# Two more pairs' keys loaded in 32x32 blocks and turned by VectorE, with a new written order of all steps

## The chip, the cores and the metric

The kernel runs on one core of one Trainium2 chip. The core has a matrix engine (TensorE, PE in the profile, with its weight loads shown apart as PEld), three element engines (VectorE or DVE, ScalarE or ACT, GpSimd or POOL) and a queue engine (SyncE or SP) that issues most DMA transfers here. The five run their own instruction lists in order and wait for each other by semaphores. The metric is the device time of one execution in microseconds.

## The reference

Inputs are q, k and v of shape (4, 8, 768, 64) and two weight matrices, 512x2048 and 2048x512. For each of 4 batches the reference computes a block-sparse attention, then a Fourier mixing layer with a two-layer network on the result.

```python
k_rep = k.reshape(B, H, 12, 64, D).mean(axis=3)            # mean key of each block of 64
gate  = einsum('bhsd,bhnd->bhsn', q, k_rep)                # causal blocks only
mask  = (top 3 blocks of each query by gate) or (own block), and causal
attn  = softmax(where(mask, q @ k.T / 8, -1e9)) @ v
x     = attn with its 8 heads side by side                 # (4, 768, 512)
u     = x + real(fft(fft(x, axis=1), axis=2))
un    = (u - mean(u)) / sqrt(var(u) + 1e-6)
out   = u + maximum(un @ w_ch1, 0) @ w_ch2
```

## The kernel before

**Units of work.** Two heads of one batch make a pair; there are 16 pairs (P = 0 to 15), four to a batch. For each pair the kernel needs q and k with the 64 elements of a head along the partitions, while memory holds them with the elements along a row. It has two ways to turn them.

- By TensorE: `load` fetches a whole head in rows of 64 floats (line 282, two transfers of 192 KB), `a_tp` (steps `tk` for keys and `tq` for queries, line 297) turns it in six 128x128 transposes into PSUM, and the later steps read PSUM.
- By blocks: `load` fetches 32 rows by 32 columns at a time (line 277, four transfers of 96 KB, rows of 32 floats), so that a turn within 32x32 blocks finishes the job. For keys that turn is `k_turn` (step `kb`, line 301), a VectorE instruction in place in SBUF; for queries it is `a_q32` (step `qc`, line 326), which copies to a new tile as well.

`BLK` on line 203 says which pairs go by blocks: queries from pair 7 on, keys from pair 9 on.

**Attention of a pair.** From the turned keys VectorE takes block sums (`a_sums`, step `ks`, line 306) and `kh` spreads them for the two heads; ScalarE casts the keys to 16 bits (`a_k`, step `kc`, lines 317 and 320), GpSimd the queries (`a_q`, step `qs`). TensorE computes gate scores (`g`); VectorE turns them (`gt`), finds the top values (`gx`, nine or ten MAX8 instructions), compares (`gl`, two instructions) and turns the mask back (`gm`). From pair 7 on GpSimd writes the mask into the operand of the scores (`K`). TensorE computes six score tiles (`s`), ScalarE takes the exponentials (`e`), GpSimd cuts the diagonal (`d`), TensorE multiplies by v (`v`, line 461; `vc` casts v on GpSimd) and VectorE divides (`x`, line 472 and a product).

**Mixing of a batch.** VectorE folds the four pairs' x (`fs`, `fd`, then `f:b,0` to `f:b,3`, lines 504 to 516). TensorE multiplies by the Fourier tables along the sequence (`y`, line 531), ScalarE and VectorE copy out (`ty`, `tr`), TensorE multiplies along the features (`m`), VectorE adds x (`u`) and ScalarE scales to 16 bits (`xu`). The result is turned into the tile `unT` (`un`): in batch 0 by TensorE (`xt`) and a VectorE copy (line 602), in the other batches by DMA transposes on SP (line 605). VectorE also takes the statistics (`bn`, `nv`), GpSimd finishes them (`nr`).

**The network.** 16 steps `w` of a batch (lines 641 and 643) multiply `unT` by the first weights, `r` applies the maximum (ScalarE, every fourth on VectorE, line 651), 12 half-steps `c` (line 668) multiply by the second weights, `o` adds on VectorE and `od` stores.

**Order.** The string `ORDER` (lines 112 to 177) is a list of these steps, written out and recorded one after the other with the framework's own scheduling switched off. So it gives each engine its instruction list: an engine runs its parts of the steps in the order of the list, and a step that must wait holds up all later ones on the same engine. SP's loads and stores stand in the same list (`Lk`, `Lq`, `Lv` for keys, queries and values, `LT` and `LF` for the Fourier tables). All PSUM results come from one pool of four buffers, so a fifth result waits for the first to be read; the q and k rows as loaded have three buffers each.

Of the kernel before, what the change touches and what calls it, by code (L numbers as in the profile page):

```python
# [112 lines left out]
Lk:1 Lq:1 Lk:2 Lq:2 tk:0 ks:0 tq:0 Lq:3 Lk:3 kh:0 qc:0 iz:1 tk:1 qs:0 kc:0 g:0 ks:1 iz:0 gt:0 tq:1  # L113
kc:1 gx:0 Lq:4 Lv:0 Lk:4 Lv:1 kh:1 gl:0,0 tk:2 gl:0,1 gm:0 kc:2 qc:1 s:0,3 s:0,2 ks:2 e:0,3 qs:1
tq:2 Lq:5 Lk:5 s:0,5 qc:2 g:1 e:0,5 e:0,2 kh:2 s:0,4 gt:1 qs:2 s:0,0 e:0,4 gx:1 s:0,1 d:0,2 tq:3
gl:1,0 e:0,0 gl:1,1 tk:3 gm:1 e:0,1 d:0,0 qc:3 g:2 d:0,3 kc:3 d:0,5 s:1,5 gt:2 d:0,4 s:1,0 e:1,5
qs:3 ks:3 s:1,4 e:1,0 tq:4 d:0,1 gx:2 vc:0 e:1,4 s:1,3 qc:4 s:1,1 Lv:2 e:1,3 s:1,2 gl:2,0 kh:3 tk:4
gl:2,1 e:1,2 d:1,3 gm:2 g:3 d:1,4 ks:4 d:1,0 v:0 d:1,5 gt:3 vc:1 kc:4 gx:3 e:1,1 s:2,5 Lv:3 Lq:6
LF:0 Lq:7 Lk:6 Lk:7 LT:0 s:2,3 kh:4 gl:3,0 e:2,5 gl:3,1 s:2,4 e:2,3 d:1,1 x:0 tq:5 qs:4 e:2,4 g:4
d:2,3 gm:3 qc:5 s:2,0 d:2,4 s:2,2 d:1,2 e:2,0 gt:4 d:2,5 tk:5 vc:2 gx:4 e:2,2 s:2,1 ks:5 d:2,0 Lv:4  # L120
Lq:8 Lk:8 s:3,1 e:2,1 v:1 gl:4,0 kh:5 gl:4,1 kc:5 d:2,1 gm:4 d:2,2 s:3,2 x:1 e:3,1 vc:3 g:5 e:3,2
Lv:5 Lc:0 d:3,1 s:3,5 gt:5 s:3,0 fs:0,1 e:3,5 s:3,3 d:3,2 gx:5 e:3,0 s:3,4 fs:1,1 tq:6 gl:5,0 e:3,3
fs:0,0 v:2 gl:5,1 fs:1,0 e:3,4 d:3,3 qc:6 d:3,0 s:4,5 x:2 d:3,4 s:4,4 e:4,5 d:3,5 s:4,0 qs:5 v:3
e:4,0 gm:5 fs:2,0 fs:2,1 e:4,4 s:5,5 x:3 s:4,1 e:5,5 s:5,1 e:4,1 fd:2,0 s:4,2 s:5,0 fs:3,1 e:5,1
# [41 lines left out]
d:14,0 vc:14 v:15 w:2,13 w:2,11 r:2,13 v:14 r:2,11 w:2,6 r:2,14 w:2,0 w:2,9 w:2,2 w:2,5 r:2,9 r:2,2
# [15 lines left out]
def kernel(  # L182
# [617 lines left out]
```

## Time and profile before

| What | Value |
|---|---|
| Median of 3 runs | 292.67 us (292.5 to 293.05) |
| The profiled execution's own time | 292.97 us |
| Its span from first to last instruction | 291.2 us |
| TensorE busy | 276.6 us (95%) |
| VectorE busy | 202.9 us (70%) |
| ScalarE busy | 163.6 us (56%) |
| GpSimd busy | 116.1 us (40%) |
| Granted TensorE clock | 1.0 of full speed throughout |

The profile is one execution. Its page gives busy time by engine, the same in 40 slices, the chain of work that ended last (each piece was released by the one before it), groups of like instructions, and DMA issues. Other answers of the trace give the instructions in order of time, sums over chosen stretches, and the time from a transfer's issue to its landing. Matmuls are pipelined, so their mean duration is longer than the distance from one to the next.

### The profile page before, as it was taken

What the parts mean: (1) busy time and instruction counts of PE and PEld (TensorE: products, weight loads), DVE (VectorE), ACT (ScalarE), POOL (GpSimd) and SP (SyncE); (2) the same over time, 40 slices, a digit from 0 to 9 for tenths busy, and PEclk for the clock granted to TensorE, in tenths of its full rate; (3) what the DMA queues carried; (4) which work ended last, traced back from release to release, by engine and by line L of the source; (5) the groups of instructions that cost most, each with busy time, mean ns of one, the idle gap of its engine ahead of it and who ended that gap; (6) DMA issues with size and microseconds to landing.
All of it is one profiled execution on the core that took longest, in us unless ns stands there. A gap on an engine that the chain in (4) does not pass through costs nothing.

```text
span 291.2 us, 6585 instructions
## 1 busy us (share of the span) xinstructions
PE 276.6 (95%) x2537; PEld 169.2 (58%) x2537; DVE 202.9 (70%) x604; ACT 163.6 (56%) x205; POOL 116.1 (40%) x286
## 2 busy tenths in 40 slices
PE   8799999899998989999998999999999999999994
PEld 4466777655665465556574466656676454564642
DVE  2999999999996978977899766793566155420231
ACT  3698989865872625978577672864263401353100
POOL 2267527454888650852771798038000000003000
PEclk9999999999999999999999999999999999999999
DMA  9999999998999297259610002543000331000063
GB/s 199 278 225 228 205 200 205 221 170 155 172 174 194 65 222 131 51 123 242 109 41 2 0 7 50 146 91 146 0 2 0 37 109 36 0 2 0 0 237 127
DMA packets 118287, 33.52 MB, mean 115 GB/s; under 512 B 111024, under 2 KB 115056, under 8 KB 118256
## 3 DMA queue, kind: packets, MB, share of 16 engines
q1 hardware_dynamic: 112592, 28.47, 45.0%
q0 software_dynamic: 3664, 4.19, 8.8%
q10 hardware_dynamic: 2000, 0.44, 0.7%
q8 instruction: 20, 0.33, 0.5%
q14 instruction: 11, 0.09, 0.1%
HBM read 28.63 MB, written 6.29 MB: 120 GB/s over the span
## 4 chain that ended last, share of the span: by engine, by line
PE 68%; DVE 17%; ACT 8%; POOL 4%; issue 2%; DVEq 0%; ACTq 0%; POOLq 0%
PE c L668 24%; PE h L641 15%; PE h L643 7%; ACT pt L443 5%; PE sc L426 5%; PE av L461 4%; DVE kr L306 2%; PE yp L531 2%; PE mx L564 2%; POOL pt L449 2%; DVE q L328 2%; PE mx L565 2%; DVE mx L378 1%; PE warmps L705 1%; DVE u L578 1%
## 5 line engine op out<-in xcount | busy, mean ns | idle before, releaser
L443 ACT ACTIVATE pt<-sc 128x1024 f16<-128x1024 f32 (+1 forms) x96 | 82.8, 921 | 28.9 <-PE sc L426 19.8
L641 PE MATMUL h<-unT,w 128*128 128x512 f16 x256 | 84.8, 379 | 2.3 <-DVE hT L651 1.1
L668 PE MATMUL c<-w_sb,hT 128*128 128x512 f16 x368 | 84.0, 379 | 0.5 <-ACT hT L653 0.5
L643 PE MATMUL h<-unT,w 128*128 128x256 f16 x256 | 69.7, 272 | 0.0
L653 ACT ACTIVATE hT<-h 128x768 f16<-128x768 f32 x48 | 37.6, 809 | 51.4 <-PE h L643 51.2
L449 POOL TENSOR_SCALAR_AFFINE_SELECT pt<-pt 128x256 f16<-128x256 f16 x96 | 40.0, 444 | 49.1 <-ACT pt L443 48.6
L668 PEld LDWEIGHTS <-hT 128*128 128x128 f16 x368 | 35.4, 98 | 40.0 <-issue 1.2
L641 PEld LDWEIGHTS <-w 128*128 128x128 f16 x256 | 25.0, 97 | 29.5 <-issue 1.2
L651 DVE TENSOR_SCALAR hT<-h 128x768 f16<-128x768 f32 x16 | 15.1, 948 | 27.3 <-PE h L643 27.3
L680 DVE SCALAR_TENSOR_TENSOR u<-c,rs,u 128x512 f32<-128x512 f32 (+1 forms) x25 | 17.5, 721 | 20.3 <-PE c L668 19.2
L643 PEld LDWEIGHTS <-w 128*128 128x128 f16 x256 | 25.0, 98 | 6.0 <-issue 2.6
L224 POOL TENSOR_SCALAR_AFFINE_SELECT qk<-q 64x768 f16<-64x768 f32 (+1 forms) x25 | 21.5, 862 | 15.0 <-DVE q L328 11.0
L426 PE MATMUL sc<-qk 96*128 96x512 f16 (+3 forms) x144 | 26.2, 306 | 0.0
L224 POOL TENSOR_SCALAR_AFFINE_SELECT qk<-mt 32x160 f16<-32x160 f16 x72 | 23.1, 341 | 7.6 <-DVE mt L398 5.8
L221 POOL TENSOR_TENSOR t<-vr,rs 128x6 f32<-128x6 f32 x12 | 2.9, 242 | 54.5 <-DVE rs L621 53.8
L461 PEld LDWEIGHTS <-pt 128*128 128x128 f16 x672 | 22.4, 97 | 3.0 <-issue 0.8
L461 PE MATMUL av<-v,pt 128*128 128x65 f16 x672 | 23.2, 193 | 0.6 <-POOL v L224 0.6
L578 DVE SCALAR_TENSOR_TENSOR u<-mx,x 128x512 f32<-128x512 f32 x24 | 15.6, 687 | 8.4 <-PE mx L565 8.4
L590 ACT ACTIVATE x<-u,nm 128x512 f16<-128x512 f32 x24 | 15.7, 714 | 9.7 <-DVE nm L584 9.5
L426 PEld LDWEIGHTS <-qk 96*128 96x128 f16 x144 | 13.1, 97 | 9.9 <-issue 1.2
L421 PE MATMUL sc<-qk 64*128 64x512 f16 (+3 forms) x112 | 14.7, 306 | 1.8 <-ACT pt L443 0.8
L610 DVE BATCH_NORM_STATS2 bst<-u 128x6 f32<-128x512 f32 x24 | 16.2, 674 | 0.0
(99 smaller groups left out, 357.2 us busy)
## 6 DMA issues: line engine op xcount, KB each, us to landing
nat<-in_v_dram SPq DMA_DIRECT2D x16, 384.0 KB, 4.3
out_dram<-u SPq DMA_DIRECT2D x23, 256.0 KB, 2.7
nat<-in_q_dram SPq DMA_DIRECT2D x36, 96.0 KB, 4.0
nat<-in_k_dram SPq DMA_DIRECT2D x17, 192.0 KB, 3.4
nat<-in_k_dram SPq DMA_DIRECT2D x28, 96.0 KB, 2.8
nat<-in_q_dram SPq DMA_DIRECT2D x13, 192.0 KB, 3.6
w_sb<-in_moe_w_ch_dram POOLq DMA_DIRECT2D x2, 1024.0 KB, 10.1
w<-in_moe_w_ch_dram POOLq DMA_DIRECT2D x2, 768.0 KB, 9.0
```

Source lines behind the costliest of these rows:

```text
L224: nc.gpsimd.affine_select(out=out, in_=in_, pattern=[[0, i] for i in n], base=0, channel_multiplier=0, compare_op=ALU.is_ge, fill=0.0)
L426: nc.tensor.matmul(ps[:, e, co:co + q1 - q0], qk[0:96, e, 1, 128 * jt:128 * jt + 128], qk[0:96, e, 0, q0:q1], start=True, stop=True)
L443: nc.scalar.activation(out=d["pt"][:, o:o + 2 * n].rearrange("p (e c) -> p e c", e=2), in_=d["sc", i][:, :, 0:n], func=AF.Exp, scale=0.125)
L449: nc.gpsimd.affine_select(out=dg, in_=dg, pattern=[[0, 2], [1, 128]], base=0, channel_multiplier=-1, compare_op=ALU.is_ge, fill=0.0)
L461: nc.tensor.matmul(av[:, e, 66 * st:66 * st + 65], pt[:, co:co + 128], vv[:, e, jt, 0:65], start=(cnt == 0), stop=(cnt == 20))
L578: nc.vector.scalar_tensor_tensor(out=u_b[:, k2, :].rearrange("p (m two) -> p two m", two=2), in0=mps[:, k2, :].rearrange("p (two m) -> p t ...
L610: nc.vector.bn_stats(out=bst, in_=u_t[b, kt // 2][:, kt % 2, :])
L641: nc.tensor.matmul(hp[:, 0:512], w1s, unT[:, dt, 0:512], start=(dt == 0), stop=(dt == NDT - 1))
L643: nc.tensor.matmul(hp[:, 512:768], w1s, unT[:, dt, 512:768], start=(dt == 0), stop=(dt == NDT - 1))
L653: nc.scalar.activation(out=hT, in_=hp, func=AF.Relu)
L668: nc.tensor.matmul(c_ps[b, g[0]][:, st - g[0], :], h_t[b, it][:, 128 * st:128 * (st + 1)], w2_sb[:, it, :], start=(it == 0), stop=(it == N ...
L680: nc.vector.scalar_tensor_tensor(out=o, in0=ps, scalar=st_t[b][1][:, st:st + 1], in1=o, op0=ALU.mult, op1=ALU.add)
```

## The change

Keys of pairs 7 and 8 go by blocks as well: their four-part loads replace two-part loads, and steps `kb:7` and `kb:8` replace `tk:7` and `tk:8`. The casts and block sums of those keys then read SBUF instead of PSUM. All other computation is the same, but the whole list of steps after the first four loads stands in another order.

```diff
-    BLK = (range(7, NPAIR), range(9, NPAIR))
+    BLK = (range(7, NPAIR), range(7, NPAIR))
```

The first lines of `ORDER`, where the work on pair 0 is given, and the lines around the loads of pair 7, the first batch's `unT`, the second batch's `y` and its `unT`:

```diff
 ORDER = """
-Lk:1 Lq:1 Lk:2 Lq:2 tk:0 ks:0 tq:0 Lq:3 Lk:3 kh:0 qc:0 iz:1 tk:1 qs:0 kc:0 g:0 ks:1 iz:0 gt:0 tq:1
+Lk:1 Lq:1 Lk:2 Lq:2 Lq:3 Lk:3 tk:0 ks:0 kh:0 iz:1 iz:0 tq:0 kc:0 qc:0 g:0 tq:1 gt:0 gx:0 gl:0,0
+gl:0,1 gm:0 qc:1 tk:1 kc:1 tk:2 kc:2 ks:1 qs:0 qs:1 Lq:4 Lv:0 Lk:4 Lv:1 kh:1 s:0,1 ks:2 s:0,3 tq:2
...
+e:0,2 g:3 ks:4 e:1,4 gm:2 Lv:2 d:0,3 qs:2 d:0,4 d:0,2 vc:0 vc:1 d:0,0 d:0,1 d:0,5 Lv:3 Lq:6 LF:0
+Lq:7 Lk:6 Lk:7 LT:0 v:0 s:1,5 s:2,4 e:1,3 kc:3 tq:5 e:1,0 s:2,5 s:2,2 e:1,1 gt:3 kc:4 gx:3 gl:3,0
...
+gl:4,1 v:1 x:1 s:3,1 s:2,0 s:3,4 g:5 kc:5 s:3,3 e:3,1 e:3,4 s:3,0 qc:7 gm:4 e:2,0 tq:6 e:3,0 s:3,5
...
-fs:3,0 s:5,2 fd:2,1 e:5,0 fd:3,1 s:4,3 fd:3,0 e:5,2 tk:6 f:0,1 f:0,2 e:4,3 Lk:9 Lq:9 tk:7 f:0,3
-e:4,2 f:0,0 y:0,1 ks:7 pg:0 W:0 kc:6 y:0,0 tr:0,1 d:4,0 kc:7 d:4,4 d:4,5 ks:6 d:5,5 d:4,1 ty:0,1
-tr:0,0 s:5,3 d:5,2 s:5,4 d:4,3 kh:6 W:1 ty:0,0 m:0,2 qs:6 e:5,3 u:0,2 m:0,1 vc:4 e:5,4 m:0,0 u:0,1
-xu:0,2 d:5,4 tk:8 d:5,1 d:4,2 u:0,0 xu:0,1 d:5,0 xt:0,2 W:2 g:6 un:0,2 xu:0,0 xt:0,1 gt:6 un:0,1
-kc:8 xt:0,0 qc:8 un:0,0 qs:8 v:4 Lq:10 Lk:10 Lv:6 Lq:11 qc:7 bn:0,3 gx:6 w:0,1 gl:6,0 r:0,1 w:0,2
+d:2,2 d:3,4 d:2,0 d:3,5 d:3,0 d:2,3 d:2,4 vc:3 d:3,2 d:3,3 gl:5,1 kb:7 v:2 e:4,1 kc:7 gm:5 ks:7 v:3
...
+s:4,2 gt:6 e:5,3 m:0,0 s:5,1 xu:0,2 e:4,2 xu:0,1 xt:0,1 gx:6 e:5,1 u:0,0 xu:0,0 Lk:9 Lq:9 W:0 W:1
+d:4,0 pg:0 vc:4 d:4,4 d:5,0 qs:6 d:4,3 d:4,1 W:2 d:4,2 d:4,5 gl:6,0 gl:6,1 v:4 un:0,1 gm:6 s:6,3
+gt:7 xt:0,0 xt:0,2 s:6,1 s:6,4 x:4 e:6,3 s:6,2 e:6,2 un:0,0 un:0,2 gx:7 gl:7,0 gl:7,1 kb:8 w:0,6
...
-fs:6,1 gt:10 c:0,1,0 s:8,2 c:0,2,0 s:8,1 s:8,0 r:0,15 fs:6,0 x:7 c:0,0,1 s:9,5 c:0,1,1 fs:7,0 gx:10
-fs:7,1 fd:7,1 fs:4,0 fd:6,0 qc:11 fd:7,0 fd:6,1 f:1,1 f:1,0 f:1,2 f:1,3 y:1,1 e:9,1 e:8,4 e:8,2
+gl:9,1 gm:9 r:0,7 r:0,13 w:0,4 gl:10,0 gl:10,1 nv:0 d:6,0 qs:8 K:8 X:1 d:7,4 d:6,2 d:7,0 d:7,2 d:7,5
+vc:7 d:7,1 vc:6 qs:9 d:7,3 K:9 nr:0 v:6 kc:8 s:8,5 s:8,2 r:0,14 s:8,4 r:0,10 kc:9 v:7 r:0,4 c:0,0,0
+s:9,0 s:8,3 s:9,1 e:8,5 c:0,0,1 s:9,3 x:6 x:7 c:0,1,0 s:8,0 e:8,2 fs:6,1 c:0,1,1 fs:7,1 fs:7,0
+fd:7,0 fs:4,0 fs:6,0 fd:6,0 qc:11 fd:7,1 fd:6,1 f:1,2 f:1,0 f:1,3 f:1,1 y:1,0 tr:1,0 e:8,4 e:8,3
...
-un:1,1 un:1,2 un:1,0 od:0,3 Lk:13 Lk:14 od:0,5 Lv:12 od:0,4 Lv:13 Lk:15 Lq:15 od:0,2 w:1,0 x:9 g:12
+e:10,5 s:10,3 Lk:13 un:1,1 Lk:14 un:1,2 un:1,0 Lv:12 Lv:13 od:0,5 od:0,2 Lk:15 Lq:15 od:0,3 kb:13
...
```

More of the change, by code (lines that the diff above doesn't have):

```diff
@@ new lines @@
+r:0,6 w:0,12 e:6,1 w:0,11 w:0,2 qc:8 ks:8 gm:7 kb:9 kh:8 g:8 r:0,12 s:6,0 r:0,11 s:6,5 w:0,0 e:6,4
+r:0,2 w:0,5 w:0,8 w:0,1 e:6,5 ks:9 r:0,5 gt:8 gx:8 gl:8,0 kh:9 gl:8,1 w:0,3 bn:0,5 gm:8 qc:9 bn:0,3
+Lq:10 Lk:10 Lv:6 Lq:11 d:6,1 K:7 qs:7 d:6,4 d:5,2 d:5,4 d:6,3 X:0 d:5,3 d:6,5 d:5,5 vc:5 d:5,1 Li:0
+Lv:7 Lq:12 Lv:8 Lv:9 s:7,3 v:5 r:0,8 r:0,0 r:0,3 r:0,1 e:6,0 bn:0,1 x:5 s:7,2 e:7,3 w:0,15 g:9 s:7,4
+e:7,2 w:0,9 e:7,4 fs:5,0 s:7,5 gt:9 s:7,1 w:0,13 r:0,15 r:0,9 s:7,0 kb:10 gx:9 ks:10 qc:10 kh:10
@@ new lines @@
+w:2,3 fs:13,0 r:2,9 bn:2,3 bn:2,1 fs:12,1 bn:2,0 bn:2,4 bn:2,5 bn:2,2 nv:2 d:15,3 vc:14 d:15,1
+d:14,2 d:15,5 d:14,1 d:15,0 d:15,2 vc:15 d:14,5 d:14,3 d:15,4 nr:2 d:14,4 d:14,0 v:15 w:2,14 w:2,7
+w:2,12 r:2,14 v:14 w:2,13 r:2,3 w:2,15 w:2,11 x:15 fs:15,0 r:2,7 r:2,13 r:2,12 w:2,1 w:2,8 r:2,1
+fs:15,1 fs:13,1 x:14 fs:14,0 fs:12,0 w:2,2 w:2,10 r:2,2 r:2,8 fd:15,1 fs:14,1 fd:14,0 fd:15,0
+fd:14,1 f:3,1 f:3,2 f:3,3 y:3,1 r:2,11 w:2,6 r:2,6 c:2,0,0 c:2,2,0 f:3,0 y:3,0 r:2,15 tr:3,1 r:2,10
+c:2,2,1 ty:3,0 c:2,0,1 tr:3,0 o:2,0 ty:3,1 m:3,1 o:2,2 m:3,0 u:3,0 c:2,1,0 u:3,1 c:2,1,1 o:2,1
@@ L177 @@
+od:3,2 od:3,3 od:3,6 od:3,1 od:3,5
 """
```

93 lines of the change are left out of this document (38 added, 55 removed).

## The prediction

> **What bounds the kernel now.** First the page's head, then the sums over four stretches, cut where one batch's work hands over to the next stage.
>
> ```profile
> PE 276.6 (95%) x2537; PEld 169.2 (58%) x2537; DVE 202.9 (70%) x604; ACT 163.6 (56%) x205; POOL 116.1 (40%) x286
> ```
> ```profile
> 10.00:57.80 47.80, 43.68 (x701) 32.04 (x700) 45.43 (x155) 42.96 (x54) 25.41 (x51) 1.00 1.07 220
> 57.80:104.30 46.50, 44.06 (x419) 25.94 (x418) 41.69 (x139) 27.39 (x34) 33.36 (x74) 1.00 0.92 159
> 104.30:180.00 75.70, 73.66 (x649) 44.26 (x650) 60.29 (x184) 51.71 (x63) 42.55 (x105) 1.00 0.43 87
> 180.00:287.00 107.00, 106.98 (x732) 62.30 (x730) 50.45 (x114) 37.28 (x49) 12.33 (x41) 1.00 0.21 60
> ```
>
> After the stretch and its length come the busy times of PE, PEld, DVE, ACT and POOL, then PE's clock and the DMA share. The last stretch belongs to PE alone (106.98 of 107.00): whatever PE has left by then is paid in full, and a VectorE gain there is worth nothing. In the first two VectorE leads: 45.43 of 47.80, with 2.4 idle, and 41.69 of 46.50, with 4.8 idle. The two ends of the second stretch are hand-overs from VectorE to PE, by the instructions in order of time:
>
> ```profile
> 57.09 0.65 DVE L602 COPY unT<-xt 128x1024 f16<-128x1024 f16 x1
> 57.79 0.38 PE L641 MATMUL h<-unT,w 128*128 128x512 f16 x1 [0.20 <-DVE unT L602]
> ```
> ```profile
> 103.44 0.80 DVE L516 COPY fg<-zw 128x6 f16<-128x6 f16 x1
> 104.29 1.28 PE L531 MATMUL yp<-fs_sb,fg 128*128 128x193 f16 x13 [0.48 <-DVE fg L516]
> ```
>
> So the first `w` of batch 0 starts when the last part of `unT` is copied (57.74), and `y` of batch 1 goes on when the fold `f:1,3` is done (104.24). The time is the second hand-over plus PE's work behind it, while the later waits stay as they are. The change is costed at these two points.
>
> **The edit itself.** Rows by line, with shapes kept apart (busy time, then mean ns of one):
>
> ```profile
> L297 PE MATMUL tp<-id,nat 128*128 128x128 f32 x96 | 13.7, 285 | 0.6 <-ACT pt L443 0.3
> L301 DVE STREAM_TRANSPOSE nat<-nat 128x768 f32<-128x768 f32 x7 | 6.7, 958 | 2.1 <-ACT pt L443 2.0
> L306 DVE TENSOR_REDUCE kr<-nat 128x12 f32<-128x768 f32 x7 | 6.6, 937 | 0.1
> L306 DVE TENSOR_REDUCE kr<-tp 128x12 f32<-128x768 f32 x9 | 8.4, 936 | 0.0
> L320 ACT CAST qk<-nat 64x768 f16<-64x768 f32 x14 | 11.6, 829 | 0.3
> L320 ACT CAST qk<-tp 64x768 f16<-64x768 f32 x4 | 3.2, 795 | 0.0
> ```
> ```profile
> 9.49 1.53 PE L297 MATMUL tp<-id,nat 128*128 128x128 f32 x12
> ```
>
> Twelve transposes leave PE. Such a run took 1.53 us to the last one's end; less the pipeline's tail they cost about 1.3. VectorE gains two turns of 0.958. Neighbours overlap a little (the 0.94 reduction at 19.58 below is followed at 20.44), so two add about 1.75. Block sums cost the same (937 for 936). The four casts are 0.034 longer, 0.14 on ScalarE, covered by its idle time in the second stretch (27.39 busy of 46.50); without that cover it would be 0.14. Two fewer PSUM results pass through the four buffers; what that can spare is the 0.3 in the last column of the first row, and I take 0. In return the keys' rows are held until `kc`, not until `tk`; the load that reuses pair 7's rows is `Lk:10`, wanted only by `kb:10`, and I take 0.
>
> **VectorE up to unT.** By the written order VectorE's list up to the last `un` of batch 0 now also holds `kb:7`, `gx:6`, `gl:6`, `gm:6`, `gt:7`, `x:4` and the small `kh:7`; `qc:7` has changed places with `qc:8`, which is neutral.
>
> ```profile
> L221 DVE TENSOR_TENSOR x<-av,rcp 128x768 f16<-128x768 f32 x16 | 15.3, 958 | 0.6
> L472 DVE RECIPROCAL rcp<-av 128x12 f32<-128x12 f32 x16 | 3.6, 226 | 3.3 <-PE av L461 3.2
> L366 DVE STREAM_TRANSPOSE gt<-g 128x160 f32<-128x160 f32 x9 | 3.1, 345 | 3.9 <-PE g L354 3.8
> L398 DVE STREAM_TRANSPOSE mt<-lt 128x288 f16<-128x288 f16 x7 | 3.3, 475 | 0.2
> L221 DVE TENSOR_TENSOR lt<-lt,oth 128x108 f16<-128x108 f16 x7 | 2.0, 287 | 0.1
> L221 DVE TENSOR_TENSOR ltb<-gt,mx 128x120 f16<-128x120 f32 x9 | 2.9, 319 | 0.1
> ```
> ```profile
> 19.58 0.94 DVE L306 TENSOR_REDUCE kr<-tp 128x12 f32<-128x768 f32 x1
> 20.44 0.71 DVE L378 MAX8 mx<-gt 128x8 f32<-128x8 f32 x9
> ```
>
> 0.96 (turn) + 0.71 + 2 x 0.29 + 0.48 + 0.35 + 0.96 + 0.23 = 4.27, with `kh:7` about 4.4; less the overlap (0.08 for each of the long ones) I take +4.1.
>
> The start costs more. Before, while PE computed `g:0`, VectorE summed the keys of pair 1; now `ks:1` stands behind `gm:0` and `qc:1`:
>
> ```profile
> 8.64 0.95 DVE L306 TENSOR_REDUCE kr<-tp 128x12 f32<-128x768 f32 x1
> 9.62 0.48 DVE L361 STREAM_TRANSPOSE gt<-g 128x288 f32<-128x288 f32 x1
> ```
>
> VectorE will stand idle from 8.64 to 9.62 and do the 0.86 of `ks:1` later: +0.9.
>
> Then the keys' landing. `kb:7` and `qc:7` now come early. SP's list in order of time, then the last part's own time to landing:
>
> ```profile
> 28.32 3.52 SPq L277 DMA_DIRECT2D nat<-in_q_dram  x4
> 31.88 2.89 SPq L282 DMA_DIRECT2D nat<-in_k_dram  x4
> 34.81 0.54 SPq L749 DMA_DIRECT2D fs_sb<-c_FS  x1
> ```
> ```profile
> L277 SPq DMA_DIRECT2D nat<-in_q_dram x1: 1461/1461/1461, 30.4 to 30.4; - x1
> ...
> DMA to landing us min/median/max: 4.2/4.2/4.2
> ```
>
> Queries of pair 7 landed at 30.4 + 4.2 = 34.6. The keys' two issues become four: from 33.7 at 0.88 each the last starts at 36.3 and lands near 40.5. VectorE did `gl:5,1` at 35.30 before; with `qc:7` and the later start put ahead it would come to `kb:7` at about 37.2 and wait up to 3.3. Against that, SP stood waiting between the values' loads `Lv:2` and `Lv:3` for `vc:1`, which now follows `vc:0` at once, so SP may run up to 2 us earlier. Between 0 and 3.3 I take +1.0, nearer the low end. The Fourier table behind these loads (`LT`, 34.81) moves by the two extra issues, 1.8 at most; the first `y` that reads it moves by more, because `kb:7` and `ks:7` (1.9 together) now stand ahead of the fold it needs, so 0. `LF` is ahead of them, and nothing else on SP's list up to there has changed its place.
>
> Of the 2.4 us that VectorE stood idle some is taken up by the new waits: -0.6. Sum: `unT` at 57.74 + 4.1 + 0.9 + 1.0 - 0.6 = 63.1.
>
> **PE up to there.** PE's list gains four score tiles of pair 6 and `g:7` ahead of the first `w`, about 4 x 0.4 + 0.4 (a score tile is four products in the row below, a gate product eight), and loses the 1.3 of transposes: it has 0.7 more to do while `unT` is 5.4 later. That alone is a wait that PE has not now.
>
> ```profile
> 62.62 0.40 PE sc L421 x4
> ...
> 89.86 0.41 PE g L354 x8
> ```
>
> **From unT to y of batch 1.** Here VectorE does `kb:8` (0.87) and both `gl:10` (at most 0.32 each) more, against 4.1 already done: up to `f:1` it carries +2.2 in all, so the stretch holds 41.69 - 1.9 = 39.8. Its idle time, 4.8, was mostly short waits; the longest goes:
>
> ```profile
> 93.86 0.23 DVE L472 RECIPROCAL rcp<-av 128x12 f32<-128x12 f32 x1 [1.86 <-PE av L461]
> ```
>
> `x:6` now has four more microseconds of VectorE work ahead of it, and PE's list up to `v:6` is as long as it was. With 0.8 of the short waits gone too, 2.1 is left: `y` goes on at 63.1 + 39.8 + 2.1 = 105.0, against 104.3: +0.7.
>
> **Behind it.** PE's list up to that `y` lacks `c:0,2,0` (1.73), `s:8,1` and `s:9,5` (0.54 together) and the transposes (1.3), and holds `s:9,0` and `s:9,3` (0.86) more: 2.7 less. As the total is only 1.3 less, 1.4 more lies behind `y`.
>
> ```profile
> 94.26 1.73 PE c L668 x8
> ```
>
> Sum: 0.7 + 1.4 = +2.1. The profiled execution's 292.97 gives 295.1; it stands 0.3 over the median of its runs (292.67), so I forecast a median of 294.8.
>
> **A rule of the skill against a row.** Mean packet time from two stretches, one with rows of 256 bytes and one with rows of 128 (11 to 15 and 110 to 113 us; packets, MB, share of 16 engines):
>
> ```profile
> q1 hardware_dynamic: 4411, 1.11, 122.6%
> ...
> q1 hardware_dynamic: 3944, 0.50, 104.1%
> ```
>
> 16 x 4 x 1.226 / 4411 = 17.8 ns and 16 x 3 x 1.041 / 3944 = 12.7 ns. A pair's keys need 1536 packets of the first or 3072 of the second: 1.71 or 2.44 us of all engines, 0.7 more a pair at a DMA share of 1.07; this lies inside the +1.0 above. The Trainium skill, page "DMA: Bandwidth & Descriptors", section "Why small descriptors are slow (HBM only)", gives a packet a fixed cost of about three cycles beside one for each 32 bytes, 7 cycles for 128 bytes against 11 for 256. By that rule, an estimate, the same bytes take 1.27 times as long; the rows say 1.43, so it speaks against the change, and not strongly enough.
>
> **Rivals.** *PE takes the gain (faster).* VectorE's idle 2.4 and 4.8 hold all that is added and both hand-overs come in time: then only the 1.3 on PE counts, 291.4. This decides if `unT` is done by 59.8 and `y` goes on by 102.9. For it speaks that 7.2 idle is more than the 2.2 added; against it that the added work stands ahead of `unT`, where only 2.4 is idle. *Nothing to be seen.* Half of that: 292.1 to 293.2. *The keys come late.* SP runs no earlier and `kb:7` waits the full 3.3, with the short waits unchanged: 2.3 and 0.8 more, 297.9. *The second `unT` comes late.* SP's key loads `Lk:13` and `Lk:14` now stand before and between its DMA transposes.
>
> ```profile
> 110.37 2.17 SPq L277 DMA_DIRECT2D nat<-in_k_dram  x4
> 113.97 11.90 SPq L605 DMA_TRANSPOSE unT<-x  x6
> ```
> ```profile
> 127.96 0.38 PE h L641
> ```
>
> The last transpose was issued by 125.9 and PE began the next `w` at 127.96, so there is no slack. One such load between costs 2.2, less 0.9 more PE work now ahead of the `w`: +1.3, 296.1. I take 0 because the four issues can go out while SP waits for `xu`.
>
> **How the numbers follow.** The forecast case, 293.3 to 296.6, has a chance of 0.50; late keys 0.12, late second `unT` 0.10, PE's gain 0.20, nothing 0.08. A difference of 0.2% (0.6 us) is about what a measurement here can tell. Slower: 0.50 + 0.12 + 0.10 = 0.72; same 0.08; faster 0.20. The range goes from the faster rival's 291.4 to 298.6, the late keys with all of VectorE's idle time kept.
>
> **What the next profile would show.** The copies of `unT` (line 602) end near 63, not 57.74; PE's wait for them exceeds 0.2; VectorE idles near 8.7 and before the turn of line 301 near 38; `y` of batch 1 goes on near 105; PE is unbroken from 180 on. It is wrong if `unT` is done before 60, or if VectorE's idle time up to `y` is under 3 us.

## The result, and the profile after

| | Before | Changed |
|---|---|---|
| Median of 7 runs each | 292.51 us | 291.65 us (290.94 to 292.08) |
| The profiled execution: own time, span | 292.97, 291.2 us | 292.08, 290.3 us |
| Ratio of the times | | 0.9961, 95% interval 0.9945 to 0.9977 |

The changed kernel was 0.4% faster where 0.7% slower was forecast. Two later runs of the same kernel, told below, came out level with the kernel before (1.0001 and 1.0006): the gain of 0.9 us is not seen every time, and the forecast loss of 2.1 us is seen in none. The ratios leave disturbed runs out (the medians are of all runs), and the first profile of the edit alone, at a granted clock of 0.978, is not read.

The head of the page of the changed kernel, and its sums over four stretches, cut at the same two hand-overs (stretch, length, then busy PE, PEld, DVE, ACT, POOL, clock, DMA share, GB/s):

```profile
PE 274.3 (94%) x2525; PEld 167.7 (58%) x2525; DVE 203.0 (70%) x606; ACT 164.4 (57%) x205; POOL 113.2 (39%) x286
```
```profile
10.00:65.30 55.30, 46.10 (x737) 32.57 (x735) 52.18 (x178) 43.37 (x53) 23.72 (x46) 1.00 1.05 204
65.30:104.80 39.50, 39.47 (x366) 23.55 (x363) 36.03 (x119) 30.11 (x37) 30.02 (x70) 1.00 0.93 157
104.80:180.00 75.20, 75.11 (x670) 46.23 (x668) 61.45 (x186) 48.95 (x60) 42.73 (x106) 1.00 0.51 105
180.00:287.00 107.00, 106.80 (x730) 61.88 (x727) 49.09 (x112) 38.19 (x50) 14.28 (x47) 1.00 0.19 53
```

The first stretch has grown from 47.8 to 55.3 us and PE stands idle in it for 9.2 (before 4.1). The second has shrunk from 46.5 to 39.5. What matters is PE's column against the length from there on: idle 0.03, 0.09 and 0.20 us where it was 2.44, 2.04 and 0.02. In the changed kernel PE hardly stops once it has begun the first `w`.

The two hand-overs, in order of time:

```profile
63.88 1.28 DVE L602 COPY unT<-xt 128x1024 f16<-128x1024 f16 x2
```
```profile
65.35 0.39 PE L641 MATMUL h<-unT,w 128*128 128x512 f16 x1
```
```profile
104.38 0.55 DVE L221 TENSOR_TENSOR fg<-zw 128x762 f16<-128x762 f16 x1
```
```profile
104.69 0.76 PE L531 MATMUL yp<-fs_sb,fg 128*128 128x193 f16 x7
```

`unT` is done at 65.2, 7.4 us later than before, and the first `w` starts 7.6 later. But the fold of batch 1 ends at 104.9, only 0.7 later, and `y` has no bracket: PE does not wait for the fold any more. PE's last product ends at 287.12 against 287.50.

Where the time came from is seen in PE's waits behind the first `w`, here of the kernel before those over 0.2 us (the one at 104.29 stands in the prediction; the bracket is the idle time and its releaser) and then the only one over 0.1 that the changed kernel has:

```profile
62.62 0.40 PE L421 MATMUL sc<-qk 64*128 64x384 f16 x4 [0.31 <-DVE kr L306]
88.40 0.38 PE L641 MATMUL h<-unT,w 128*128 128x512 f16 x1 [1.11 <-DVE hT L651]
103.12 0.68 PE L531 MATMUL yp<-fs_sb,fg 128*128 128x193 f16 x6 [0.53 <-DVE fg L513]
140.81 0.38 PE L641 MATMUL h<-unT,w 128*128 128x512 f16 x1 [0.35 <-ACT pt L443]
156.96 0.38 PE L641 MATMUL h<-unT,w 128*128 128x512 f16 x1 [0.43 <-ACT hT L653]
159.32 1.89 PE L668 MATMUL c<-w_sb,hT 128*128 128x512 f16 x8 [0.47 <-ACT hT L653]
173.48 1.44 PE L461 MATMUL av<-v,pt 128*128 128x65 f16 x42 [0.61 <-POOL v L224]
```
```profile
185.53 0.81 PE L668 MATMUL c<-w_sb,hT 128*128 128x512 f16 x3 [0.20 <-ACT pt L443]
```

A bracket shows less than a wait costs, since a modelled end covers part of it. Taken from start to start, as what each product's distance to the next exceeds the median of its kind, the waits behind the first `w` were 6.3 us and are 0.8. The account from profile to profile: first `w` +7.56; PE's time from there to its end 229.71 before and 221.77 after, -7.94, of which 5.5 are these waits; the rest, 2.4, is put down to the four score tiles and the gate product that now stand ahead of the `w` (about 2.0 in the prediction's sum). The transposes stand ahead of it in both kernels. Sum -0.38 at PE's end. The span shrank by 0.95; the other 0.57 lie behind PE's last product. From PE's end to the end of the span the three profiles with the old list and the old `BLK` (before, and n1 and n2 below with one step moved) took 3.72 us, the seven that have the edit and the changed kernel's list from the first `w` to the `y` of batch 2 took 3.15 to 3.17, and the others 3.41 to 3.47, while in all of them the last store's data had been moved 1.9 us behind PE's end. So this part goes with the kernel, and it is more than half of the gain in the profile; no run looks for its cause.

### The profile page after: what moved, and what is told of

Same layout as the page of the kernel before. It is cut to its first block, busy times and chain, and to the rows that moved or that the text cites. A ratio compares the mean times of both kernels' runs of the same rounds, so it can differ in the third digit from the quotient of the medians.

```text
span 290.3 us, 6581 instructions
## 1 busy us (share of the span) xinstructions
PE 274.3 (94%) x2525; PEld 167.7 (58%) x2525; DVE 203.0 (70%) x606; ACT 164.4 (57%) x205; POOL 113.2 (39%) x286
## 4 chain that ended last, share of the span: by engine, by line
PE 79%; DVE 13%; ACT 5%; issue 2%; DMA 1%; DVEq 0%; ACTq 0%
PE c L668 27%; PE h L641 19%; PE h L643 10%; PE sc L426 7%; PE av L461 4%; ACT pt L443 4%; DVE u L578 2%; PE yp L531 2%; DVE kr L306 2%; DVE q L328 2%; PE warmps L705 1%; PE sc L421 1%; DVE mx L378 1%; PE c L660 1%; PE g L354 1%
## 5 line engine op out<-in xcount | busy, mean ns | idle before, releaser
L668 PE MATMUL c<-w_sb,hT 128*128 128x512 f16 x368 | 83.0, 379 | 0.2 <-ACT pt L443 0.2
L449 POOL TENSOR_SCALAR_AFFINE_SELECT pt<-pt 128x256 f16<-128x256 f16 x96 | 38.5, 424 | 68.0 <-ACT pt L443 45.9
L224 POOL TENSOR_SCALAR_AFFINE_SELECT v<-nat 128x768 f16<-128x768 f32 x16 | 14.7, 920 | 8.6 <-DMA nat<-in_v_dram 8.6
L544 ACT CAST ty<-yp 128x772 f16<-128x772 f32 x8 | 8.0, 1036 | 16.7 <-PE yp L531 16.4
```

The source lines that it names most:

```text
L224: nc.gpsimd.affine_select(out=out, in_=in_, pattern=[[0, i] for i in n], base=0, channel_multiplier=0, compare_op=ALU.is_ge, fill=0.0)
L449: nc.gpsimd.affine_select(out=dg, in_=dg, pattern=[[0, 2], [1, 128]], base=0, channel_multiplier=-1, compare_op=ALU.is_ge, fill=0.0)
L668: nc.tensor.matmul(c_ps[b, g[0]][:, st - g[0], :], h_t[b, it][:, 128 * st:128 * (st + 1)], w2_sb[:, it, :], start=(it == 0), stop=(it == N ...
```

## The experiments

All of them change `BLK` or the list `ORDER`, and compute the whole reference. From the traces, in us; "y to end" is PE's time from the first `y` of batch 1 to its last product:

| Kernel | unT done | first w | first y of batch 1 | y to end | median | before, beside it |
|---|---|---|---|---|---|---|
| before | 57.7 | 57.8 | 103.1 | 184.4 | 292.51 | |
| changed | 65.2 | 65.4 | 104.7 | 182.4 | 291.65 | 292.51 |
| e1b edit alone | 59.5 | 59.6 | 105.6 | 184.0 | 294.75 | 292.67 |
| e2 order alone | 69.3 | 70.7 | 115.3 | 182.4 | 303.04 | 292.67 |
| h1 old, then new from first w | 57.9 | 64.0 | 104.2 | 182.9 | 292.94 | 292.67 |
| h2 new, then old from first w | 64.3 | 63.7 | 111.0 | 183.9 | 300.18 | 292.67 |
| h3 new, then old from first y | 64.1 | 64.3 | 107.5 | 183.6 | 296.40 | 292.67 |
| k1 new, then old from y of batch 2 | 65.7 | 65.9 | 105.3 | 183.5 | 293.38 | 292.67 |
| k2 old, then new from y of batch 2 | 59.5 | 60.4 | 105.6 | 185.5 | 296.38 | 292.67 |
| e2c order alone, keys later | 64.9 | 66.7 | 111.3 | 184.4 | 300.94 | 292.66 |
| e2d the same, cast near | 65.0 | 66.4 | 106.6 | 184.2 | 296.00 | 292.64 |
| n1 before, one step later | 57.7 | 57.8 | 103.1 | 188.8 | 297.07 | 292.66 |
| n2 before, one step earlier | 57.1 | 57.2 | 102.5 | 183.6 | 292.19 | 292.64 |
| c1 changed, gap covered | 64.9 | 65.1 | 104.5 | 182.5 | 292.66 | 292.66 |
| a2 changed again | 66.0 | 66.2 | 105.5 | 182.8 | 292.99 | 292.65 |
| a3 changed, beside l1 | 66.2 | 66.4 | 105.8 | 182.7 | 293.10 | 292.99 |
| l1 changed, one table later | 64.1 | 64.3 | 103.6 | 182.5 | 291.47 | 292.99 |

### The edit alone, the order alone

The edit in the old list, in place:

```diff
-    BLK = (range(7, NPAIR), range(9, NPAIR))
+    BLK = (range(7, NPAIR), range(7, NPAIR))
-... f:0,2 e:4,3 Lk:9 Lq:9 tk:7 f:0,3 ... u:0,1 xu:0,2 d:5,4 tk:8 d:5,1 ...
+... f:0,2 e:4,3 Lk:9 Lq:9 kb:7 f:0,3 ... u:0,1 xu:0,2 d:5,4 kb:8 d:5,1 ...
```

> The edit without the new order: the written order of the kernel before, with the two turns on VectorE exactly where TensorE's transposes of the keys of pairs 7 and 8 stood. VectorE's list up to unT of batch 0 grows by two turns (about 1.75 us), TensorE loses 1.3 us. Slack theory (a later first w is paid back, because TensorE's waits behind it shrink by as much): between 1.3 faster and no change, 291.2 to 292.5. Order theory (the waits behind the first w are gone only because the new list behind it is better): 1.75 - 1.3 = 0.5 slower, 293.0. Turns theory (only the 1.3 on TensorE counts, the order does nothing): 291.2.

> The edit alone in the old list once more, for a profile at full clock: 294.2 to 294.9; the second w or the y of batch 1 late by what the two turns add on VectorE, 1.0 to 2.0 us, and TensorE waiting for VectorE there.

294.68 us in the first run (ratio 1.0063, 1.0041 to 1.0084) and 294.75 in the second (1.0069, 1.0047 to 1.0091): the edit by itself costs 2.1 us. The first run's time is 1.7 over the highest of its three theories (293.0). The second run's profile has `unT` 1.8 later, about the two turns of 0.96 that VectorE got, and two waits of PE that were not there at this size, one for ScalarE, which scales what VectorE delivers, and one for VectorE:

```profile
57.10 0.40 PE L597 MATMUL xt<-id,x 128*128 128x128 f16 x4 [1.36 <-ACT x L590]
65.63 0.38 PE L641 MATMUL h<-unT,w 128*128 128x512 f16 x1 [1.10 <-DVE x L221]
```

The turns stand in VectorE's list ahead of what PE waits for, so they are paid; the 1.3 us that PE saves are not gained, since PE only waits longer.

The new list without the edit:

```diff
-    BLK = (range(7, NPAIR), range(7, NPAIR))
+    BLK = (range(7, NPAIR), range(9, NPAIR))
-... gl:5,1 kb:7 v:2 e:4,1 kc:7 ... gl:7,1 kb:8 w:0,6 ...
+... gl:5,1 tk:7 v:2 e:4,1 kc:7 ... gl:7,1 tk:8 w:0,6 ...
```

> The new order without the edit: keys of pairs 7 and 8 go by TensorE again, its transposes standing where the two turns stand in the changed kernel. TensorE has 1.3 us more than in the changed kernel, VectorE two turns less, 0.87 of it ahead of unT. Slack and order theories: about 1 us over the changed kernel, 292.2 to 293.0. Turns theory: as the kernel before, 292.5.

303.04 us (ratio 1.0342, 1.0306 to 1.0379), 10 us over what any of the theories allowed. Each half is slower than the kernel before and both together are not, so the two are no sum. What holds the second back is taken up with e2c and e2d below.

### Which stretch of the list brings the gain

Four kernels carry the edit and change lists at one point; k1 stands for the form:

```diff
-ORDER = new
+i = new.index("y:2,1")
+ORDER = new[:i] + [s for s in old if s not in new[:i]]
```

h1 takes the steps that the new list has ahead of its first `w` in their old sequence (the two turns a few steps later than in the edit alone), and then the new list; h2 the steps that the old list has ahead of its first `w` in their new sequence, and then the old list; h3 the same with the first `y` of batch 1 as the point; k2 is k1 with old and new changed over.

> The edit with the steps that the new list has ahead of its first w put in the sequence of the old list, and the new list from there on. The first w of batch 0 should start some microseconds earlier than 65.4. Order theory: the early start is kept and the waits behind stay away, the changed kernel less the earlier start, 287 to 289. Slack theory: TensorE's waits come back behind the first w, 291 to 292.

> The edit with the steps that the old list has ahead of its first w put in the sequence of the new list, and the old list from there on. The first w starts later than 57.8. Order theory: the old list's waits behind it (4.5 us of TensorE idle from 57.8 to 180) come on top of the later start, 294 to 298. Slack theory: a later start is paid back by shorter waits, 291 to 293.

> The steps ahead of y of batch 1 stand in the new sequence, everything behind it in the old one; the edit is in. Theory Stretch: each list removes the waits of TensorE in its own stretch, and the old list behind that y brings back its own, 3.0 us in the profile of before (at 127.96, 140.8, 149.7, 156.9, 159.3 and 173.5) against 0.6 after: y of batch 1 as in the changed kernel at 104.5 to 105.2, total 293.6 to 294.6. Rival Carry: what the new list does ahead of y gives the later stages their slack, so the old list behind it is as good: 291.4 to 292.2.

> New list until the second y of batch 2, old list behind it. Theory Stretch: TensorE had no wait worth speaking of behind that point before (0.2 us) and has none after; only the end behind TensorE's last product differs (3.7 against 3.2 us): 291.6 to 292.3, TensorE without a break from 180 on. Rival Late: part of the gain lies in the last two batches, 292.8 or more.

> Old list with the edit in it until the second y of batch 2, new list behind it. Theory Stretch: the old list has lost its time by then, so this stands at the edit alone, 294.0 to 294.7. Rival Late: the new list behind it gives the gain, 292.5 or less.

h1 has `unT` done 7.3 us earlier than the changed kernel, yet its first `w` starts only 1.4 earlier, because the four score tiles ahead of it wait for their masks:

```profile
60.51 0.37 PE L433 MATMUL sc<-mt,indz 64*128 64x160 f16 x8 [1.73 <-DVE mt L398]
61.53 0.48 PE L354 MATMUL g<-q,krb 128*32 128x160 f32 x8 [0.65 <-DVE rcp L472]
```

Behind that `w` it has no wait but two of 0.28 and 0.19, and PE ends at 287.13, as in the changed kernel (287.12). That is one execution, of 292.10 us; the twelve ran from 291.76 to 300.06, and their median of 292.94 (ratio 1.0011, 0.9981 to 1.0040) is no gain over the kernel before and meets neither theory's number. What its profile shows is where the waits are: the new sequence of the head is not what takes them away; the list from the first `w` on is. h2 shows the reverse: with the old list behind it a first `w` that is 4.1 us later than in e1b ends 5.4 later. A late first `w` is not paid back by itself, so the theory that the old waits were slack falls; the 300.18 us are 2.2 over the other theory's range too. In h3 the waits behind the `y` come back, with the very idle times of the kernel before, 3.7 us later:

```profile
144.49 0.38 PE L641 MATMUL h<-unT,w 128*128 128x512 f16 x1 [0.35 <-ACT pt L443]
160.63 0.38 PE L641 MATMUL h<-unT,w 128*128 128x512 f16 x1 [0.43 <-ACT hT L653]
162.99 1.89 PE L668 MATMUL c<-w_sb,hT 128*128 128x512 f16 x8 [0.47 <-ACT hT L653]
177.15 1.44 PE L461 MATMUL av<-v,pt 128*128 128x65 f16 x42 [0.61 <-POOL v L224]
```

They are a property of the old list, whatever ran ahead of it. My numbers for h3 and k2 were missed, by 1.7 us or more: around the point where the lists meet each got waits of its own (in h3 1.21 us at 98.05 and 1.00 at 105.82, in k2 1.50 at 180.20). Pieces of two lists do not fit without loss, so these runs place the gain but do not price each stretch. k1 (291.91 to 295.58, and one of 298.14) has one wait of 0.43 at the point and one of 0.16 behind it. Its median is 1.1 over what its first theory allows; in its profile VectorE had waited 2.71 us for the keys of pair 7, a matter of the head that comes below.

### One wait by itself

n1 and n2 take the kernel before and its wait at 173.48 for GpSimd's copy of the values of pair 12.

```diff
-... f:2,0 f:2,3 nr:1 d:12,0 ... d:12,3 qs:15 d:12,5 d:12,4 d:12,2 vc:12 ...
+... f:2,0 f:2,3 d:12,0 ... d:12,3 qs:15 d:12,5 d:12,4 nr:1 d:12,2 vc:12 ...
```

> The kernel before with one step moved: nr:1, which stood ahead of the masks of pairs 12 and 13 on GpSimd, behind d:12,4. It tests one of the waits behind y of batch 1 by itself: 0.77 us of TensorE at 173.48, for GpSimd's v. Theory Stretch: the wait goes and nothing takes its place, as TensorE is unbroken from 180 on: 291.9 to 292.2 against 292.67. Rival: the wait was set by the values' transfer or by the masks themselves, and stays: 292.5 to 292.8.

4.4 us slower (297.07; 1.0145, 1.0113 to 1.0177). I had misread the row: in the kernel before GpSimd did the twelve small instructions of `nr:1` while the exponentials of pair 12 were still to come. Behind `d:12,4` they fall into no such pause and stand ahead of the copy that PE wants (first and last of the twelve, then the copy):

```profile
171.66 0.20 POOL L221 TENSOR_TENSOR t<-vr,rs 128x6 f32<-128x6 f32 x1
...
174.75 0.20 POOL L221 TENSOR_TENSOR rs<-rs,t 128x6 f32<-128x6 f32 x1
...
175.25 0.90 POOL L224 TENSOR_SCALAR_AFFINE_SELECT v<-nat 128x768 f16<-128x768 f32 x1
```
```profile
176.21 2.36 PE L461 MATMUL av<-v,pt 128*128 128x65 f16 x42 [3.38 <-POOL v L224]
```

```diff
-... f:2,3 nr:1 d:12,0 ... d:12,2 vc:12 d:13,0 ...
+... f:2,3 vc:12 nr:1 d:12,0 ... d:12,2 d:13,0 ...
```

> The kernel before with one step moved: vc:12, GpSimd's copy of the values of pair 12, ahead of nr:1 (where GpSimd stood idle for 7.0 us ahead of 161.05) instead of behind the masks of pair 12; the changed kernel has it further forward still. Theory Stretch: TensorE's wait at 173.48 for that copy goes and is not replaced: 292.0 to 292.2 against 292.67. Rival: the masks, 0.9 earlier at most, hold the product instead and less than 0.3 is won: 292.4 or more.

The wait is gone, and the product follows the one before it at its own pace:

```profile
172.09 1.45 PE L461 MATMUL av<-v,pt 128*128 128x65 f16 x42
```

PE's time from the first `y` to its end went from 184.38 to 183.62, by 0.76, which is what the wait took from start to start (0.77; the bracket said 0.61). The median is 0.45 lower (ratio 0.9987, 0.9969 to 1.0005: in itself at the edge of what can be told). In this stretch a wait of PE is paid in full, and the step to take it away is one copy at another place in the list.

### Why the new order needs the edit

In e2 VectorE waited 6.5 us ahead of the block sums of pair 7:

```profile
40.91 0.88 PE L297 MATMUL tp<-id,nat 128*128 128x128 f32 x6 [0.33 <-ACT pt L443]
```
```profile
44.11 1.59 ACT L320 CAST qk<-tp 64x768 f16<-64x768 f32 x2
```
```profile
45.73 0.96 DVE L306 TENSOR_REDUCE kr<-tp 128x12 f32<-128x768 f32 x1 [6.52 <-PE av L461]
```

The transposes were done at 41.8, ahead of the products of values. The list has the cast `kc:7` ahead of the sums `ks:7`, and the sums, on another engine, started when the cast of the same PSUM result had ended (45.70); the semaphore that they waited for is ScalarE's, and the bracket names a product that ended in the same moment. The cast in turn stood on ScalarE behind an exponential that had waited for a product (43.06). The first expectation below speaks of a transpose behind a product of values and has this row wrong. In the changed kernel the same two steps stand in the same order, but the keys lie in SBUF, and the sums ran at 39.83, ahead of the cast at 43.21.

e2c puts the transposes and their readers later, e2d leaves pair 7 as in e2c and brings pair 8's cast forward:

```diff
 e2c
-... gl:5,1 kb:7 v:2 e:4,1 kc:7 gm:5 ks:7 ... kh:7 ... gl:7,1 kb:8 w:0,6 ...
+... gl:5,1 v:2 e:4,1 gm:5 ... f:0,3 tk:7 y:0,1 e:5,2 ks:7 ... kc:6 kc:7 ty:0,0 kh:7 ... g:6 tk:8 ...
 e2d, against the changed kernel at pair 8
-... gl:7,1 kb:8 w:0,6 ... w:0,2 qc:8 ks:8 ... v:6 kc:8 s:8,5 ...
+... gl:7,1 tk:8 ks:8 kc:8 w:0,6 ... w:0,2 qc:8 ... v:6 s:8,5 ...
```

> The new order without the edit, as in the order alone, but with the transposes of pairs 7 and 8 and the steps that read them put at places like those of the old list (behind the folds of batch 0 and behind g:6), so that VectorE does not wait 6.5 us for a transpose behind a product of values. Theory Order: the new list gives the gain whatever engine turns the keys; TensorE has 1.3 us more in the head and VectorE 1.9 less, unT 63 to 65, no waits worth speaking of behind the first w, total 291.3 to 293. Rival Joint: the waits behind the first w come back, because the four PSUM buffers are handed round in another phase: 294 or more.

> The new order without the edit, with pair 7's transposes as in the run before this one, pair 8's where the blocks of pair 8 are turned, and pair 8's sums and casts (ks:8, kc:8) right behind them. By the written order the transposed keys of pair 8 hold one of the four PSUM buffers until kc:8, which the new list has just ahead of s:8,5. Theory Hold: that buffer is what the two runs without the edit lacked, its lack is what made TensorE wait 1.06 us at each of several w; with kc:8 forward these waits go, y of batch 1 comes at 104.5 to 107 and the total is 291.5 to 294. Rival: the waits behind the first w belong to the transposes or to the order, and stay: 297 or more.

e2c: 300.94 us, so theory Order falls. Between the first `w` and `y` of batch 1 PE waits again and again for ScalarE to empty the result just made:

```profile
56.06 0.87 PE L297 MATMUL tp<-id,nat 128*128 128x128 f32 x6
```
```profile
69.05 0.38 PE L641 MATMUL h<-unT,w 128*128 128x512 f16 x1 [0.90 <-ACT hT L653]
77.89 0.38 PE L641 MATMUL h<-unT,w 128*128 128x512 f16 x1 [0.90 <-ACT hT L653]
80.25 0.38 PE L641 MATMUL h<-unT,w 128*128 128x512 f16 x1 [0.90 <-ACT hT L653]
```
```profile
94.42 1.61 ACT L320 CAST qk<-tp 64x768 f16<-64x768 f32 x2
```

The keys of pair 8 are turned into PSUM at 56.06, and their last reader is the cast that ends at 96.03. For 40 us they hold one of the four buffers. The second `w` (69.05) starts when ScalarE has read the result of the first (69.00), so the two have one buffer between them; and a `w` at 96.08 starts right behind the cast. With the cast at the transposes (e2d) the three waits at `w` are gone, `y` of batch 1 comes 4.7 us earlier and the time is 296.00 (ratio 1.0119, 1.0092 to 1.0145). Theory Hold is borne out for these waits; its number was too low by 2, because other waits were left, one of 0.98 at the second `w` for the cast itself and one of 1.50 at 133.61 for the DMA transposes of the second `unT`. The Trainium skill, page "Perfetto Trace Analysis", section "Optimization Strategy", says that the same gap repeated for a stretch can mean that there is not enough PSUM for the next tile. The trace agrees: start to start, the three waits are 1.062, 1.062 and 1.061 us.

So turning by VectorE does something that its instruction times don't show. The turned keys lie in SBUF, and the cast may then stand 22 us behind the turn (66.39 to 88.15 in the changed kernel) without costing PE a buffer. In the new order, whose cast stands there, the edit is worth 3 to 4 us (e2d against the changed kernel's 291.65 to 293.10), though e2d need not be the best list without it; in the old order, where the cast is near, it costs 2.1.

### The head: the gap at the start, and the rows of pair 7

```diff
-... iz:0 tq:0 kc:0 qc:0 g:0 tq:1 gt:0 ... gm:0 qc:1 tk:1 kc:1 tk:2 kc:2 ks:1 qs:0 ...
+... iz:0 tq:0 kc:0 qc:0 tk:1 g:0 ks:1 tq:1 gt:0 ... gm:0 qc:1 kc:1 tk:2 kc:2 qs:0 ...
```

> The changed kernel with the keys' sums of pair 1 put back behind the first gate product, where the kernel before has them, so that VectorE does not stand idle for 0.90 us at 9.52. Theory Head: behind the first w TensorE runs without a break, so the time is the start of that w plus a fixed 221.8 us and unT is held by VectorE; unT 0.5 to 0.9 earlier, total 290.7 to 291.2 against the changed kernel's 291.65. Rival Elsewhere: VectorE meets the same gap at the next wait of the head (0.60 at 42.20, 0.83 at 50.36), unT stays at 65.0 to 65.3 and the total at 291.4 to 291.9.

The gap of 0.90 is filled, and `unT` is done only 0.2 earlier than in the first profile of the changed kernel; 292.66 us, ratio 0.9996 (0.9970 to 1.0022), over both numbers expected. VectorE met other waits, which the first profile didn't have:

```profile
35.16 0.98 DVE L326 STREAM_TRANSPOSE q<-nat 128x768 f32<-128x768 f32 x1 [1.67 <-DMA nat<-in_q_dram]
40.15 0.98 DVE L301 STREAM_TRANSPOSE nat<-nat 128x768 f32<-128x768 f32 x1 [1.03 <-DMA nat<-in_k_dram]
```

These are the late rows of pair 7 that the prediction had set between 0 and 3.3 us. In the first profile of the changed kernel the turn of line 301 has no bracket. So the changed kernel was run again.

> The changed kernel once more, on another chip beside the kernel before. Three kernels with its list behind the first w (h1, k1 and c1) ran at 291.0 to 292.4 in half of their executions and at 292.8 to 300 in the others, where the kernel before stays within 292.2 to 293.1 in nearly all. Theory Clock: with TensorE unbroken from the first w on, the granted clock falls below 1.0 in some executions and the list is more exposed to it: lowest 290.9 to 291.3, half of the executions over 292.4, median 291.7 to 293. Rival: those three are slower for their own steps, and the changed kernel stays at 290.9 to 292.1 in all, median 291.5 to 291.8.

292.99 us (291.57 to 293.23, and one of 296.75), ratio 1.0001 (0.9987 to 1.0016). The turn of the first profile, and then the two waits of this one:

```profile
38.57 0.98 DVE L301 STREAM_TRANSPOSE nat<-nat 128x768 f32<-128x768 f32 x1
```
```profile
36.04 0.98 DVE L326 STREAM_TRANSPOSE q<-nat 128x768 f32<-128x768 f32 x1 [2.21 <-DMA nat<-in_q_dram]
41.17 0.98 DVE L301 STREAM_TRANSPOSE nat<-nat 128x768 f32<-128x768 f32 x1 [1.29 <-DMA nat<-in_k_dram]
```

SP's four issues of pair 7's queries, first profile and repeat, and the sums from 20 to 30 us in the same order (DMA share and GB/s stand last):

```profile
27.17 4.15 SPq L277 DMA_DIRECT2D nat<-in_q_dram  x4
```
```profile
29.10 3.68 SPq L277 DMA_DIRECT2D nat<-in_q_dram  x4
```
```profile
20.00:30.00 10.00, 7.70 (x132) 5.09 (x126) 9.59 (x34) 6.69 (x9) 5.74 (x11) 1.00 1.15 257
```
```profile
20.00:30.00 10.00, 9.30 (x154) 6.47 (x150) 9.48 (x39) 8.07 (x11) 6.46 (x12) 1.00 1.08 230
```

The DMA engines were busy throughout in both (a share over 1), and where they moved 230 GB/s instead of 257 the issue came 1.9 us later. The first profile is the exception: the other seven profiles of kernels with the edit and the new head (in c1 and l1 with a step or two moved) moved 222 to 237 GB/s in this stretch, and VectorE waited 0.95 to 3.5 us for pair 7 in each of them. That the first profile had no such wait was luck. The clock was 1.00, and the two shortest executions of this run had 0.994. The median fits theory Clock, but a falling clock is not what this shows; theory Landing took its place, and l1 tests it by moving one load of 384 KB that is wanted late, with the changed kernel (a3) beside it on the same chip:

```diff
-... Lv:3 Lq:6 LF:0 Lq:7 Lk:6 Lk:7 LT:0 v:0 ...
+... Lv:3 Lq:6 Lq:7 Lk:6 Lk:7 LT:0 LF:0 v:0 ...
```

> The changed kernel with one load moved: LF:0, a Fourier table of 384 KB that is wanted only at about 53 us, behind the rows of pair 7 and LT:0 instead of ahead of them. In the repeat of the changed kernel VectorE waited 2.21 us for the queries of pair 7 and 1.29 for its keys (none in the first profile, 2.71 and 2.70 in two others). Theory Landing: these waits make the changed kernel's spread; with 384 KB less ahead of them, about 1.6 us at 230 GB/s, they shrink by 1 to 2.5 in sum, and the median lies 0.3 to 1.0 under that of the changed kernel beside it, 291.0 to 292.2, with a smaller spread. Rival: the waits are covered by others of the head, as the gap at g:0 was, and the two medians agree within 0.2.

> The changed kernel beside the run with the table later, as its measure: 291.5 to 293.2 in single executions, median 291.6 to 293.0; VectorE waits for the rows of pair 7 for 0 to 3.5 us ahead of line 326 and line 301, and the execution's time follows that wait.

a3: 293.10 (ratio 1.0006, 0.9986 to 1.0026), with waits of 1.76 and 1.22 at the same two lines. l1: 291.47 (290.70 to 293.26), ratio 0.9965 (0.9945 to 0.9985) to the kernel before, 1.6 us under a3, more than the 0.3 to 1.0 expected. Of the two waits one is left:

```profile
38.36 0.98 DVE L301 STREAM_TRANSPOSE nat<-nat 128x768 f32<-128x768 f32 x1 [0.95 <-DMA nat<-in_k_dram]
```

2.03 us of wait are gone (1.76 + 1.22 - 0.95) and `unT` is 2.2 earlier. These waits are not all that `unT` hangs on: the first profile of the changed kernel had neither, and its `unT` came 1.1 later than l1's. Four of l1's twelve runs still lie at 292.8 to 293.3, at a granted clock of 0.994, though two of its shorter ones had that clock too; what makes this rest of the spread stays open. On one chip l1 beats both kernels, and it is the only version that was run beside both.

## Why the prediction was wrong

**The step that failed** is the sentence that "the later waits stay as they are". Behind the first `y` of batch 1 the prediction counted 1.4 us more work and nothing else. The work came as counted, and the waits went: PE's time from that `y` to its end fell from 184.38 to 182.43, by 1.95, while its waits there fell from 3.8 to 0.6 from start to start; so the work grew by 1.3. In sum, that `y` came 1.6 later, the work behind it grew by 1.3 and the waits shrank by 3.2: -0.4 at PE's end where +2.1 was forecast. The other 0.57 of the shorter span lie behind PE's end, which the forecast had also left as it was; their cause is open. h1 and h3 show that these waits belong to the old list from that point on. By the brackets most of them hang on the places of ScalarE's exponentials and maxima and of GpSimd's copy, and n2 took one of them away by itself and won its full price. I had costed the change at two points, though the whole list had been written anew, and every one of the waits between 104 and 180 had a row in the trace of before that a look at the new list could have followed. For `v` of pair 12 that look would have found `vc:12` ahead of the diagonal cuts of pair 11.

**The start gap** was right: 0.90 us at the same turn. It was not to be had by covering it (c1).

**The landing of pair 7** was set at +1.0 between 0 and 3.3. It was 0 in the first profile, and 3.5 and 3.0 in the two repeats, where PE's end came 1.1 and 1.3 later and the gain was gone. The bounds were nearly right, though much of the wait was for the queries (2.21 and 1.76), which were not counted; that the term differs so much between executions was not seen. The rival of the late keys had the right mechanism, but not its 297.9, which stood on the same failed step.

**VectorE up to unT**: 63.1 was predicted and 65.2 came. Its idle time grew by 1.5 (7.82 to 9.34), near the 1.3 of the sum; its busy time grew by 5.9 (49.9 to 55.8) where 4.1 was counted. The two instructions `lt` took 1.66 us more in sum with one more of each, and the sums' spread `kh` 0.88 more with as many as before: some small instructions lasted three to five times as long as in their row (below).

**From unT to y**: 105.0 was predicted for the fold and 104.9 came, by two errors that cancel. `unT` was 2.05 later, and the stretch 39.8 instead of 41.9 us: VectorE had 36.0 us of work in it, 3.8 less than I counted, and 3.5 of idle time, 1.4 more. Why its work was that much less was not taken apart.

**PE's waits** that should show it: PE's idle time ahead of the first `w` grew by 5.1, near the 4.7 (5.4 less 0.7) of the step "PE up to there". The wait for `unT` itself does not exceed 0.2; the idle time lies further ahead, at the products that `unT` comes from.

**The rivals.** "PE takes the gain" gave 291.4, next to the measured 291.65, and is nevertheless wrong: it asked for `unT` by 59.8 and `y` by 102.9, which came at 65.2 and 104.7. The second `unT` was not late in the changed kernel; its mechanism showed in e2d (1.50 us).

**Twelve transposes fewer** were costed at 1.3 us of PE and nothing for PSUM buffers. In the old list the 1.3 bought nothing (e1b). The buffer, put at 0, cost about 5 us where the new list had to do without it (e2c against e2d), and the wait of one reader of a PSUM result for the other, not in the sum at all, 6.5 us of VectorE's time in e2.

## What to carry to other kernels

Where a change rewrites the order of an in-order kernel, follow every wait of the engine that bounds it through the new list, one by one, and not just the hand-overs that the edit touches; a wait on that engine was paid in full here (n2), and its size from start to start is more than the bracket shows. A result that stays in PSUM until its last reader takes a buffer for all that time, and its readers on two engines may wait for each other, so price a transpose by where its readers stand as well as by its instructions. A term that is a race between full DMA queues and an engine should keep both its ends in the forecast, and is worth a second profile before a small gain is believed.

## What the runs showed of the hardware

Small VectorE instructions with two inputs in SBUF that started while GpSimd ran a select lasted until that select, or an unbroken row of them, ended. Two of VectorE's in the changed kernel, and GpSimd's beside the first:

```profile
26.40 0.93 DVE L221 TENSOR_TENSOR lt<-gt,mx 128x108 f16<-128x108 f32 x1
...
33.18 0.27 DVE L221 TENSOR_TENSOR lt<-gt,mx 128x108 f16<-128x108 f32 x1
```
```profile
26.32 0.91 POOL L224 TENSOR_SCALAR_AFFINE_SELECT v<-nat 128x768 f16<-128x768 f32 x1 [0.97 <-DMA nat<-in_v_dram]
```

The first ends at 27.33, when GpSimd's select, to 27.23, has just ended; at 33.18, with GpSimd idle from 32.45 to 35.41, the same instruction takes 0.27. A `kh` at 54.02 took 1.42 and ended at 55.44; GpSimd's selects ran without a pause from 52.29 to 55.40. The Trainium skill, page "SBUF — State Buffer", section "SBUF: two separate sides", has a port pair that the two share by an exclusive lock, where whichever started first holds it for its whole instruction, so that a VectorE instruction with two inputs in SBUF is blocked by a GpSimd instruction that reads SBUF; the rows agree. No run here was made for it, so that it accounts for the whole of the 1.8 us that VectorE's work came out too long is argued from the rows and not shown.

The DMA rate with all 16 engines busy differed between executions of one kernel, 257 and 230 GB/s from 20 to 30 us (222 in a3), and a term of the forecast was 0 us in the first and 3.5 in the second.
